# Three more units of w_out's product in rounded parts, and a new order of issue, in a fused attention and feed-forward kernel

## The chip, the core and the metric

The kernel runs on one core of a Trainium2 chip. The metric is the device time of one execution in microseconds (us). Before the change it was 151.05 us, the median of three runs (150.78 to 151.63). The engines are named as the profile names them: PE is TensorE, DVE is VectorE, ACT is ScalarE, POOL is GpSimd and SP is SyncE, which here issues every transfer.

## The reference

Two stages follow each other. The first is a linear attention with quadratic features, for 4 batches and 4 heads of 1088 tokens with 32 values each:

```python
phi(x) = outer(S1 @ x, S2 @ x)                    # 8 x 8 = 64 features
kv  = einsum('bhsf,bhsd->bhfd', phi(k), v);  z = phi(k).sum(tokens)
x   = (phi(q) @ kv) / (phi(q) @ z + 1e-6)         # heads side by side: 128 values a token
h    = relu(x @ w_in)                             # 1024 wide
conv = sum(conv_w[k] * h shifted by k - 1 tokens, k = 0, 1, 2)
out  = (h * sigmoid(conv)) @ w_out                # back to 128
```

[...]

## The kernel before

**The work.** All the tokens stand side by side, 4 x 1088 with a column of zeros between the batches, and are cut into nine segments (`SEGS`: 382, seven of 510, 404 columns). Each segment meets eight blocks of 128 of the 1024 hidden values, so there are 72 units, and the last two blocks of the last segment are halved: 74 units (`UNITS`), numbered segment by segment. Unit 8s + f is block f of segment s up to unit 69; 70 and 71 are the halves of block 6 of the last segment, 72 and 73 those of block 7.

**A unit** is a chain over the engines:

- `f_in:u` (PE, L1190 to L1192): three matmuls with rounded parts (whi by xhi, wlo by xhi, whi by xlo) into the PSUM bank `a`
- `f_relu:u` (ACT L1198 or DVE L1200): the ReLU, from `a` to `h` in SBUF
- `f_tapa:u`, `f_tapb:u` (DVE, L1204): the two outer taps of the convolution, added into `a`
- `f_gate:u` (ACT, L1211): the sigmoid
- `f_mul:u` (POOL, or DVE; L1215): `g` = `h` times the gate
- `f_out:u` (PE): `g` by a block of `w_out`, added up in the bank `o` over the eight units of a segment

`f_out` has two forms. The plain one (L1240) is one fp32 matmul, which the profile shows as two instructions. For the units in `THREE`, blocks 1, 4 and 6 (`PARTS`) of the segments 3 to 7, ACT first rounds `g` (`f_hi`, L1219), POOL takes the rest (`f_lo`, L1223), and PE runs three matmuls with rounded parts (L1230 to L1232): 15 units. After the eighth unit `f_copy` brings `o` to SBUF and `f_store` sends it out.

**Before the units** the attention makes `x`. Batch 0 goes by tokens: `q_ab:0:g`, `q_take`, `q_ac`, `q_sum`, `q_rec`, `q_div`, `q_phi` (POOL, L877), the transposes `q_t` (PE), `q_ttake`, then `q_x:0:1` (PE, L1148), whose result becomes `xhi` and `xlo` by `q_hi:0:0` and `q_lo:0:0` (DVE, L1166). The first `f_in` needs `q_lo:0:0`. The batches 1 to 3 go by features, through DRAM rows (`r_put`, `rep`) and products on POOL (`q_prod`, L1136). The weights are taken apart in quarters (`i:0` to `i:3` for `w_in`, `o:0` to `o:3` for `w_out`: the steps `low`, `e`, `m`, `f`, `clamp`, `power`, `sign`, `value`, and for `w_in` also `high` and `rest`).

**What sets the order.** The table `ORDER` (L86) writes out by hand, for every engine, the order of its steps, and so also which engine takes a step that two could take. Instructions of an engine are issued in that order and in no other. A planner, `schedule` (L488), goes through the table with costs and deals out buffers of a few pools by it (seven PSUM banks `p`, six `row` buffers and so on); it also puts in four warm-up matmuls ahead of PE's first step. SP issues a transfer once the eighth one before it has landed. The planner's guess of when a load lands (`landed`, L551 to L556) so enters the buffers dealt out and the sequence in which the engines' streams are recorded, but not the order within an engine.

Of the kernel before, what the change touches and what calls it, by code (L numbers as in the profile page):

```python
# [56 lines left out]
    for b in range(B)  # L57
# [40 lines left out]
        k_ab:1:0 k_ab:0:0 k_ab:1:1 s:turn k_ab:0:1 k_z:1 q_b:1 k_wz:1 k_ab:0:2 q_a:1 k_z:0 k_kv:0:0 k_wz:0 q_den:1
        k_f:3 k_kv:0:1 q_ab:0:0 k_ab:3:1 q_ab:0:1 k_f:2 k_kv:0:2 k_kv:1:0 k_kv:1:1 k_kvt:0 q_all:1 q_t:0:0:1 q_t:0:0:0
        k_ab:3:0 k_ab:2:1 q_t:0:1:1 q_t:0:1:0 q_ab:0:2 k_ab:2:0 k_kvt:1 q_x:0:1 k_z:2 k_kv:3:0 q_b:2 f_in:2 f_in:0  # L100
        f_in:3 k_wz:2 f_in:7 k_kv:3:1 q_a:2 f_in:1 q_t:0:2:0 f_in:6 q_t:0:2:1 q_den:2 k_kv:2:0 k_kv:2:1 q_x:0:2 f_in:4
# [12 lines left out]
    """,
    "ACT": """
        s:low i:0:low k_take:0:0 i:0:clamp i:0:power i:3:low k_wq:1 k_take:0:2 q_atake:1 i:3:clamp i:0:high i:3:power
        k_wq:0 o:0:clamp i:1:low o:0:power k_ftake:3 i:1:clamp i:3:high i:1:power q_take:0:0 k_take:3:1 oh:1:high
        q_take:0:1 k_ftake:2 i:1:high k_kvtwo:0 o:3:low i:2:low o:3:clamp o:3:power k_kvtake:0 i:2:clamp i:2:power
        q_ttake:0:0:0 k_take:3:0 k_take:2:1 o:2:low q_ttake:0:1:1 q_ttake:0:1:0 oh:6:high q_take:0:2 k_take:2:0
        k_kvtake:1 o:2:clamp q_hi:0:0 o:2:power q_btake:2 f_relu:2 f_relu:0 f_relu:3 k_wq:2 o:1:low f_relu:7 k_kvtwo:3  # L120
        f_gate:0 k_kvturn:3 i:2:high f_gate:2 f_relu:1 q_ttake:0:2:0 f_gate:3 q_eps:2 q_ttake:0:2:1 f_relu:6 f_gate:1
        f_gate:7 q_hi:0:2 f_relu:4 o:1:clamp f_relu:5 o:1:power f_gate:6 f_relu:14 f_gate:4 f_relu:8 f_gate:5
        f_relu:10 f_relu:9 f_gate:8 f_relu:13 oh:4:high f_relu:12 f_gate:9 k_kvtwo:2 k_kvtake:3 f_gate:10 f_copy:0:0
        f_gate:13 f_relu:11 f_gate:14 k_kvturn:2 q_hi:1:2 q_hi:1:3 q_hi:1:1 q_hi:1:0 f_gate:12 f_relu:15 f_gate:11
        f_relu:26 f_relu:25 f_relu:18 f_gate:15 f_relu:20 f_relu:17 f_relu:16 f_gate:26 f_gate:17 f_gate:16 f_relu:21
        f_gate:18 f_gate:25 f_relu:30 f_relu:19 f_gate:20 f_copy:1:0 f_relu:22 f_relu:23 f_gate:19 f_gate:21 f_hi:25
# [1197 lines left out]
```

## Time and profile before

| | |
|---|---|
| median of three runs | 151.05 us (150.78 to 151.63) |
| the profiled execution | 150.91 us |
| its span in the trace | 149.2 us |
| what lies around the span | 1.7 us |
| instructions on PE, DVE, ACT, POOL | 1116, 278, 252, 152 |
| PE clock granted | 1.0 |

The span is what the profile's rows show, from the first instruction to the last; the runs' times are some 1.7 us longer. Start times in the rows count from the span's start. Busy times of PE overlap, since matmuls are pipelined, so that the step from one start to the next tells more than a duration; for the other engines a step is some 0.1 us shorter than a duration.

### The profile page before, as it was taken

The page shows a single profiled execution, that of the slowest core. Times are in us where ns is not written, and L with a number is a line of the kernel's source. Part 1 is how long each engine was busy: PE and PEld are TensorE (multiplying, and loading weights), DVE is VectorE, ACT ScalarE, POOL GpSimd, SP SyncE. Part 2 cuts the span into 40 slices and gives each one's busy share as a digit, 9 for nine tenths or more (in the row PEclk, how much of TensorE's full clock was granted, in tenths as well). Part 3 has the DMA queues.
Part 4 walks back from the last instruction along what each step waited for, and adds up shares of the span by engine and source line. Part 5 has one row for each costly group of instructions (what it writes and reads, how often), then busy time and mean ns, then how long its engine had stood idle before and what let it go on. Part 6 is the DMA issues. An engine that isn't in the chain of part 4 may idle for free.

```text
span 149.2 us, 3306 instructions
## 1 busy us (share of the span) xinstructions
PE 143.1 (96%) x1116; PEld 96.1 (64%) x1116; DVE 136.9 (92%) x278; ACT 117.0 (78%) x252; POOL 135.4 (91%) x152
## 2 busy tenths in 40 slices
PE   7998897999999999999999999999999999999991
PEld 3486686776765486564547655765676776686780
DVE  1789999999999999999999999999999999999910
ACT  4054979799977986979797888799898898898621
POOL 7858999999999999998999989999999999999810
DMA  4999999699992670001339217700200010020021
GB/s 114 301 324 405 407 406 399 241 253 256 228 239 70 187 165 0 4 20 50 70 91 251 78 40 190 179 0 0 70 4 0 5 67 0 2 70 0 0 74 55
DMA packets 9233, 19.82 MB, mean 133 GB/s; under 512 B 1280, under 2 KB 5376, under 8 KB 9216
## 3 DMA queue, kind: packets, MB, share of 16 engines
q1 hardware_dynamic: 9216, 19.61, 43.3%
q8 instruction: 9, 0.15, 0.4%
q14 instruction: 8, 0.07, 0.2%
HBM read 15.70 MB, written 3.90 MB: 131 GB/s over the span
## 4 chain that ended last, share of the span: by engine, by line
PE 81%; DMA 10%; SPq 3%; ACT 3%; issue 0%; ACTq 0%
PE o L1240 31%; PE a L1190 12%; PE a L1191 11%; PE a L1192 11%; DMA rows<-in_w_in 5%; DMA vt<-in_v 5%; PE xps L1148 3%; PE o L1230 3%; PE o L1231 2%; PE o L1232 2%; PE qps L1022 2%; SPq L643 2%; PE kvps L968 1%; SPq L646 1%; PE qps L1076 1%; ACT e L762 1%
## 5 line engine op out<-in xcount | busy, mean ns | idle before, releaser
L1204 DVE SCALAR_TENSOR_TENSOR a<-h,ratio,a 128x510 f32<-128x510 f32 (+3 forms) x148 | 94.8, 706 | 0.4 <-ACT h L1198 0.2
L1215 POOL TENSOR_TENSOR g<-h,s 128x510 f32<-128x510 f32 (+3 forms) x57 | 68.3, 1222 | 3.7 <-PE o L1240 2.5
L1240 PE MATMUL o<-g,w_out_sb 128*128 128x510 f32 (+2 forms) x130 | 52.2, 517 | 0.0
L1211 ACT ACTIVATE s<-a,mid 128x510 f32<-128x510 f32 (+3 forms) x57 | 37.5, 666 | 6.5 <-DVE a L1204 4.7
L1198 ACT ACTIVATE h<-a 128x512 f32<-128x512 f32 (+3 forms) x71 | 39.0, 569 | 4.4 <-PE a L1192 2.2
L1190 PE MATMUL a<-xhi,whi 128*128 128x512 f32 (+3 forms) x74 | 37.4, 505 | 0.0
L1240 PEld LDWEIGHTS o<-g,w_out_sb 128*128 128x128 f32 x130 | 23.3, 189 | 9.8 <-issue 5.1
L1191 PE MATMUL a<-xhi,wlo 128*128 128x512 f32 (+3 forms) x74 | 28.0, 379 | 0.0
L1192 PE MATMUL a<-xlo,whi 128*128 128x512 f32 (+3 forms) x74 | 28.0, 378 | 0.0
L1190 PEld LDWEIGHTS a<-xhi,whi 128*128 128x128 f32 x74 | 13.9, 188 | 10.3 <-ACT s L1211 2.8
L1223 POOL TENSOR_TENSOR gg<-g,gg 128x510 fp32r<-128x510 f32 x15 | 19.2, 1288 | 0.6 <-ACT gg L1219 0.3
L1191 PEld LDWEIGHTS a<-xhi,wlo 128*128 128x128 f32 x74 | 14.0, 189 | 5.6 <-issue 3.5
L1136 POOL TENSOR_TENSOR rows<-rows 128x544 f32<-128x544 f32 x12 | 16.2, 1364 | 0.0
L1192 PEld LDWEIGHTS a<-xlo,whi 128*128 128x128 f32 x74 | 13.9, 188 | 2.5
L877 POOL TENSOR_TENSOR kp<-kab 128x768 f32<-128x768 f32 (+2 forms) x6 | 11.7, 1958 | 2.6 <-ACT kab L615 1.7
L1211 ACT ACTIVATE a<-a,mid 128x510 f32<-128x510 f32 (+3 forms) x17 | 10.5, 623 | 1.8 <-DVE a L1204 1.8
L1215 DVE TENSOR_TENSOR g<-h,a 128x510 f32<-128x510 f32 (+3 forms) x17 | 10.6, 626 | 0.7 <-PE o L1240 0.6
L1219 ACT CAST gg<-g 128x510 fp32r<-128x510 f32 x15 | 9.4, 627 | 0.2 <-DVE g L1215 0.2
L1230 PE MATMUL o<-gg,ohi 128*128 128x510 f32 x15 | 8.7, 578 | 0.0
L615 ACT COPY out<-o 128x510 f32<-128x510 f32 (+2 forms) x10 | 5.2, 524 | 4.3 <-PE o L1240 4.3
L732 ACT ACTIVATE f<-rows 128x256 f32<-128x256 uint32 x7 | 3.1, 448 | 4.3 <-DMA rows<-in_w_in 4.2
L717 PE MATMUL warm<-w_out_sb 128*128 128x512 f32 x8 | 5.4, 838 | 1.1 <-POOL above L676 1.1
(127 smaller groups left out, 178.7 us busy)
## 6 DMA issues: line engine op xcount, KB each, us to landing
...
```

The source lines that it names most:

```text
L877: e.tensor_tensor(out=out.rearrange("p c (h i j) -> p (c h) i j", i=R, j=R), in0=a.unsqueeze(3).broadcast_to([P, n, R, R]), in1=b.unsqueez ...
L1136: mul(on["q_prod", b, pr, c])(out=st["rep", 0][:, pr, cols], in0=st["rep", 0][:, pr, cols], in1=st["rep", 1][:, pr, cols], op=ALU.mult)
L1190: nc.tensor.matmul(a[:, : n + 2], whi[:, w], xhi[:, x], start=True, stop=False)
L1191: nc.tensor.matmul(a[:, : n + 2], wlo[:, w], xhi[:, x], start=False, stop=False)
L1192: nc.tensor.matmul(a[:, : n + 2], whi[:, w], xlo[:, x], start=False, stop=True)
L1198: nc.scalar.activation(h[:, : n + 2], a[:, : n + 2], AF.Relu)
L1204: nc.vector.scalar_tensor_tensor(out=a, in0=h[:, k : n + k], scalar=ratio[:, f, k : k + 1], in1=a, op0=ALU.mult, op1=ALU.add)
L1211: nc.scalar.activation(s, a, AF.Sigmoid, scale=mid[:, f : f + 1])
L1215: mul(on["f_mul", u])(out=gt[:, :n], in0=st["h"][:, 1 : n + 1], in1=st["s"], op=ALU.mult)
L1223: mul(on["f_lo", u])(out=gg[:, 1], in0=st["g"][:, :n], in1=gg[:, 0].bitcast(F32), op=ALU.subtract)
L1230: nc.tensor.matmul(to, ohi[:, i], gg[:, 0], start=f == 0, stop=False)
L1240: nc.tensor.matmul(acc[g, p][:, : hi - lo], w_out_sb[:, f * P : (f + 1) * P], st["g"][:, lo - c0 : hi - c0], start=f == 0, stop=f == NF - 1,)
```

## The change

It has three parts.

**Three more units in rounded parts.** `THREE` now begins at segment 2, so the units 17, 20 and 22 (510 columns each) get an `f_hi` and an `f_lo`, and their `f_out` has the three-matmul form: 18 units in all.

**The planner's guess.** A load that the planner takes to be through between 16.5 and 30 us counts as landed 0.6 us later. No instruction comes from this alone.

**A new order.** All five lists of `ORDER` are new; the steps are the same but for the three `f_hi` and `f_lo`. Forty-two steps change engines. DVE takes over eight `f_mul` (8, 13, 29, 30, 51, 58, 64, 72) and gives POOL five (9, 43, 62, 65, 67); it takes five `f_relu` (23, 31, 50, 67, 69) and gives ACT three (24, 33, 66); it takes `i:0:low`, `i:1:low`, `i:3:low`, `o:2:low`, `q_atake:1`, `q_eps:2`, `k_take:3:0`, `k_kvtake:1` and the last `f_copy`, and gives ACT or POOL `k_take:1:0`, `s:take`, `o:0:low`, `q_btake:1`, `q_atake:2`, `q_hi:0:1`, `q_ttake:0:0:1`, `q_eps:1`, `q_eps:3`, `k_wq:3` and `oh:4:rest`. The units are no longer begun in the same sequence within a segment, and on SP the loads of `v3` and `o2` come earlier, those of `i2` and `v2` later. The line numbers of what follows `ORDER` are two higher (L1204 is now L1206).

```diff
     "SP": """
-        dma:k2 dma:v1 dma:o3 dma:i2 r_put:1:0:b dma:v2 dma:o2 dma:q0.2 r_put:1:3:b dma:v3 dma:q2 r_put:1:2:b
+        dma:k2 dma:v1 dma:o2 dma:o3 dma:v3 r_put:1:3:b r_put:1:2:b dma:q0.2 dma:i2 r_put:1:0:b dma:q2 r_put:1:1:b
...
-THREE = [u for u, (s, f, c0, n) in enumerate(UNITS) if f in PARTS and 3 <= s < NSEG - 1]
+THREE = [u for u, (s, f, c0, n) in enumerate(UNITS) if f in PARTS and 2 <= s < NSEG - 1]
...
-            landed.append(wire + 450)
-            lat = wire + 450 - t
+            there = wire + 450 + 600 * (16500 < wire < 30000)
+            landed.append(there)
+            lat = there - t
```

Three places show how the lists moved. The first is DVE's stream behind the preparation of the small weights (`ratio` is its last result). `kab<-kps` is a `k_take`, `kp<-kab,kps` is `k_phi:1:1`, and the rows of 128x256 take `w_in` apart. Before:

```order
L847 TENSOR_TENSOR ratio<-small,least 128x24
L615 COPY kab<-kps 128x320
L739 TENSOR_SCALAR e<-rows 128x256
L744 TENSOR_SCALAR m<-rows 128x256
L747 SCALAR_TENSOR_TENSOR f<-m,f 128x256
L615 COPY kab<-kps 128x2x128
L767 SCALAR_TENSOR_TENSOR w<-rows,e 128x256
L615 COPY s2t<-s_213 128x128
```

And with the change:

```order
L849 TENSOR_TENSOR ratio<-small,least 128x24
L617 COPY kab<-kps 128x2x128
L879 TENSOR_TENSOR kp<-kab,kps 128x1024
L746 TENSOR_SCALAR m<-rows 128x256
L617 COPY kab<-kps 128x2x96
L741 TENSOR_SCALAR e<-rows 128x256
L736 TENSOR_SCALAR f<-rows 128x256
```

The first copy on DVE is now the shorter `k_take:1:1`, the outer product follows it at once, and a `low` step (L736) stands on DVE where ACT had it; the copy of 320 columns and that of `s2t` are gone from DVE.

The second place is the end of DVE's stream. `g<-h,a` is an `f_mul` on DVE, `h<-a` an `f_relu`; 404 columns belong to whole units of the last segment, 202 to its halves. Before, the last rows are:

```order
L1204 SCALAR_TENSOR_TENSOR a<-h,ratio,a 128x404
L1204 SCALAR_TENSOR_TENSOR a<-h,ratio,a 128x202 x2
L1215 TENSOR_TENSOR g<-h,a 128x404
L1204 SCALAR_TENSOR_TENSOR a<-h,ratio,a 128x202
L1215 TENSOR_TENSOR g<-h,a 128x404
L1215 TENSOR_TENSOR g<-h,a 128x202
```

With the change they are:

```order
L1217 TENSOR_TENSOR g<-h,a 128x404
L1202 TENSOR_SCALAR h<-a 128x406
L1206 SCALAR_TENSOR_TENSOR a<-h,ratio,a 128x202
L1206 SCALAR_TENSOR_TENSOR a<-h,ratio,a 128x404
L1217 TENSOR_TENSOR g<-h,a 128x202
L1206 SCALAR_TENSOR_TENSOR a<-h,ratio,a 128x404
L1206 SCALAR_TENSOR_TENSOR a<-h,ratio,a 128x202 x3
L1217 TENSOR_TENSOR g<-h,a 128x404
L1217 TENSOR_TENSOR g<-h,a 128x202
L617 COPY out<-o 128x202
```

In both, the product of 404 columns that stands last but one among the products is `f_mul:69`, and the one of 202 columns behind it is `f_mul:73`; the last `f_relu` is now `f_relu:69`, a few rows ahead of it, and the copy of a finished half to the output has come to DVE behind everything else. PE's list ends in both with `f_out:69` and then the four halves.

The third place is SP's list of transfers behind the load of `k2` (`in_kT`, 128x1088). Before:

```order
L636 DMA vt_73<-in_v 128x1152
L646 DMA rows<-in_w_out 128x512
L646 DMA rows<-in_w_in 128x512
L1118 DMA far<-r 32x3x272
L636 DMA vt_74<-in_v 128x1152
L646 DMA rows<-in_w_out 128x512
L643 DMA rows<-in_qT 128x320
L1118 DMA far<-r 32x3x272
L636 DMA vt_75<-in_v 128x1152
L643 DMA rows<-in_qT 128x1088
```

With the change:

```order
L638 DMA vt_73<-in_v 128x1152
L648 DMA rows<-in_w_out 128x512 x2
L638 DMA vt_75<-in_v 128x1152
L1120 DMA far<-r 32x3x272 x2
L645 DMA rows<-in_qT 128x320
L648 DMA rows<-in_w_in 128x512
L1120 DMA far<-r 32x3x272
L645 DMA rows<-in_qT 128x1088
```

`q0.2` (`in_qT`, 128x320) had one quarter of `w_in` ahead of it that it no longer has, and one more `r_put`; `q2` (`in_qT`, 128x1088) no longer has `v2` (`vt_74`) ahead of it. `v2` now follows `q3`.

More of the change, by code (lines that the diff above doesn't have):

```diff
@@ L96 @@
+        f_store:6:0 f_store:7:0 f_store:8:0 f_store:8:1
     """,
     "PE": """
[L98 to L101, printed above, removed]
@@ L117 @@
[L117 to L121, printed above, removed]
@@ L122 @@
[L122 to L126, printed above, removed]
@@ L137 @@
-        f_relu:61 f_gate:72 f_relu:67 f_gate:64 f_relu:63 f_gate:61 f_relu:69 f_gate:67 f_relu:73 f_relu:70 f_gate:63
-        f_gate:69 f_gate:73 f_gate:70 f_copy:7:0 f_copy:8:1 f_copy:8:0
+        s:low k_take:1:0 k_take:0:0 s:take i:3:clamp i:3:power i:0:clamp q_btake:1 k_wq:1 o:0:low i:0:power k_take:0:2
+        o:0:clamp o:0:power i:0:high k_wq:0 i:1:clamp k_ftake:3 i:3:high i:1:power oh:1:high q_take:0:0 k_take:3:1
+        q_take:0:1 q_eps:1 i:1:high k_ftake:2 k_kvtwo:0 o:3:low o:2:clamp o:2:power o:3:clamp k_kvtake:0 o:3:power
@@ new lines @@
+        k_take:2:0 q_ttake:0:0:1 k_kvturn:1 q_ttake:0:0:0 q_ttake:0:1:1 q_ttake:0:1:0 k_take:2:1 i:2:low q_take:0:2
+        q_hi:0:0 i:2:clamp q_hi:0:1 i:2:power oh:6:high o:1:low q_btake:2 f_relu:0 f_relu:3 k_wq:2 f_relu:7 f_relu:1
+        f_gate:0 f_gate:3 oh:4:high k_kvtwo:3 q_atake:2 k_kvturn:3 f_relu:6 q_ttake:0:2:1 f_relu:2 f_gate:7 i:2:high
+        q_ttake:0:2:0 f_gate:1 f_gate:6 o:1:clamp k_kvtwo:2 o:1:power q_hi:0:2 k_kvtake:3 f_relu:5 f_gate:2 f_relu:4
+        k_kvturn:2 f_relu:8 f_gate:5 f_relu:9 f_gate:4 f_relu:14 f_relu:11 f_relu:13 f_gate:8 f_relu:12 f_gate:14
@@ new lines @@
+        f_gate:9 f_copy:0:0 q_hi:1:2 q_hi:1:3 f_gate:12 f_relu:10 f_gate:11 f_relu:15 k_wq:3 f_gate:10 q_hi:1:1
+        q_hi:1:0 f_gate:13 q_btake:3 q_atake:3 f_gate:15 f_relu:24 f_relu:17 f_relu:20 f_relu:16 f_gate:24 f_relu:18
+        f_gate:17 f_gate:20 f_relu:19 f_gate:16 f_hi:17 f_gate:18 f_relu:26 f_hi:20 f_copy:1:0 f_relu:22 f_gate:19
+        f_relu:21 q_eps:3 f_gate:23 f_relu:27 f_gate:22 f_relu:25 f_gate:21 f_gate:27 f_relu:30 f_hi:22 f_relu:28
+        f_gate:25 f_gate:26 k_kvtake:2 f_gate:30 q_hi:2:1 q_hi:2:0 f_relu:29 f_gate:28 f_hi:25 f_copy:2:0 f_relu:34
@@ L139 @@
     """,
     "DVE": """
-        s:m s:e s:f s:clamp s:power s:sign s:value taps k_take:1:0 i:0:e i:0:m i:0:f k_take:1:1 i:0:sign s:take
-        k_take:0:1 i:3:m k_zmask:1 i:3:f k_phi:1:1 o:0:low q_btake:1 o:0:m i:3:e k_zmask:0 q_m:1 o:0:f o:0:e i:3:sign
-        q_eps:1 i:1:e i:1:m o:0:sign i:1:f k_phi:0:2 i:1:sign q_ac:0:0 q_rec:1 q_sum:0:0 q_ac:0:1 q_rec:0:0 q_sum:0:1
-        q_div:0:0 q_rec:0:1 q_div:0:1 o:3:m o:3:e o:3:f i:2:e k_kvtwo:1 i:2:m o:3:sign q_ttake:0:0:1 i:2:sign q_div:1
-        k_phi:3:0 i:2:f o:2:e o:2:m q_ac:0:2 o:2:f q_sum:0:2 k_zmask:2 q_rec:0:2 q_lo:0:0 o:2:sign q_hi:0:1 q_div:0:2
@@ L175 @@
[L175 removed]
+        ones ident wqs s:four k_phi:1:0 k_phi:0:0 i:0:value k_phi:0:1 i:3:value o:0:value i:0:rest i:3:rest i:1:value
+        oh:1:rest q_wide:1 q_phi:0:0 q_phi:0:1 k_phi:2:0 i:1:rest o:3:value k_phi:3:1 q_phi:0:2 o:2:value i:2:value
+        f_mul:0 k_phi:2:1 f_mul:7 i:2:rest f_mul:1 f_mul:6 o:1:value f_mul:2 oh:4:rest f_mul:3 q_wide:2 oh:6:rest
+        q_prod:1:0:0 q_prod:1:1:1 q_prod:1:0:1 f_mul:14 q_prod:1:1:0 f_mul:9 f_mul:12 f_mul:11 f_mul:10 q_prod:2:0:0
```

120 lines of the change are left out of this document (62 added, 58 removed).

## The prediction

> **What bounds the kernel now.** I read the page first, then the busy times by stretch, then the chain of waits, and last the timelines of the start and the end. The page has three engines above 90%, so the whole span does not say which one binds:
>
> ```profile
> PE 143.1 (96%) x1116; PEld 96.1 (64%) x1116; DVE 136.9 (92%) x278; ACT 117.0 (78%) x252; POOL 135.4 (91%) x152
> ```
>
> The stretches do. The columns are the stretch in us, then the busy us of PE, weight loads, DVE, ACT and POOL:
>
> ```profile
> 20.00:28.20 8.20, 7.41 (x186) 5.54 (x181) 7.92 (x22) 7.51 (x23) 8.20 (x8) 1.00 1.00 386
> 28.20:60.00 31.80, 31.80 (x300) 22.10 (x297) 31.59 (x62) 27.00 (x63) 31.33 (x29) 1.00 0.69 170
> 60.00:100.00 40.00, 40.00 (x190) 24.16 (x189) 39.76 (x66) 34.08 (x65) 38.92 (x33) 1.00 0.34 91
> 100.00:143.00 43.00, 43.00 (x196) 29.52 (x195) 42.27 (x74) 37.71 (x75) 40.22 (x34) 1.00 0.06 19
> ```
>
> From 28.2 us on PE is never idle, and DVE is idle for 0.21 + 0.24 + 0.73 = 1.2 us of 114.8. POOL is idle for 0.5 + 1.1 + 2.8 = 4.3 us by the unrounded rows, ACT for 16. So two engines run without a break side by side, and the end is set by the one that has more left. At the end the timeline shows which:
>
> ```profile
> 141.49 0.57 DVE L1215 TENSOR_TENSOR g<-h,a 128x404 f32<-128x404 f32 x1
> ...
> 141.50 4.45 PE L1240 MATMUL o<-g,w_out_sb 128*128 128x510 f32 x22
> ...
> 142.64 0.37 DVE L1215 TENSOR_TENSOR g<-h,a 128x202 f32<-128x202 f32 x1 [0.58 <-PE o L1240]
> ...
> 143.37 0.61 POOL L1215 TENSOR_TENSOR g<-h,s 128x202 f32<-128x202 f32 x1 [2.01 <-PE o L1240]
> ...
> 146.04 0.33 ACT L615 COPY out<-o 128x202 f32<-128x202 f32 x1 [0.40 <-PE o L1240]
> ```
>
> DVE makes f_mul:69 at 141.49 and is done at 143.0, while PE works off 22 instructions: f_out:63, then 67, 68, 69 and the four halves. PE is the last, by a little.
>
> **The three units on PE.** The chain of waits has the price of both forms:
>
> ```profile
> 67.93 3.42 PE o L1240 x8
> ...
> 110.11 0.23 PE o L1230
> 110.35 0.23 PE o L1231
> 110.58 0.23 PE o L1232
> 110.81 0.24 PE a L1190
> ```
>
> Eight instructions in 3.42 us are four plain units, 0.855 each; the other form takes 110.81 - 110.11 = 0.70. Three units save 3 x 0.155 = 0.47 us of PE. Row against rule: the Trainium skill's page "FP8 and Floating Point Precision", section "TensorE Precision Notes", counts four passes for a true fp32 matmul; four of the 0.233 us passes would be 0.93, and the saving 0.69. The row stands, and nothing below uses 0.69.
>
> By 0.855 for f_out:63 and 0.69 for each whole unit of 404 columns (0.855 x 404 / 510 = 0.68, and a second pair), f_out:69 starts in before at 141.50 + 0.855 + 1.38 = 143.74. From there to the last copy at 146.04 are 2.30 us. Since f_out:69 and four halves end PE's list before and after, this 2.30 stays, and the question is when f_out:69 can start: when PE gets there, or when DVE has finished f_mul:69.
>
> **The same three units on POOL and ACT.**
>
> ```profile
> L1215 POOL TENSOR_TENSOR g<-h,s 128x510 f32<-128x510 f32 x45 | 57.5, 1300 | 1.4 <-ACT s L1211 0.8 <-PE o L1240 0.2
> ...
> L1223 POOL TENSOR_TENSOR gg<-g,gg 128x510 fp32r<-128x510 f32 x15 | 19.2, 1288 | 0.6 <-ACT gg L1219 0.3 <-DVE a L1204 0.3
> ...
> L1219 ACT CAST gg<-g 128x510 fp32r<-128x510 f32 x15 | 9.4, 627 | 0.2 <-DVE g L1215 0.2
> ```
>
> POOL gains 3 x 1.29 = 3.9 us. It gives DVE eight f_mul for five: six of 510 columns for three, which is 3 x 1.30 = 3.9 less, and one each of 404 and 202 for two of 404, which is some 0.4 more (half a product of 404, and the 202 above takes 0.61). oh:4:rest comes and k_kvturn:1 goes, both small. So POOL has about 0.4 more. ACT gains 3 x 0.63 = 1.9 for f_hi and loses two f_relu of about 0.6. Both lie in the idle 4.3 and 16 us, so I count them at nothing; uncovered, they would cost 0.4 and 0.7.
>
> **DVE** pays for it. Steps from start to start:
>
> ```profile
> 116.67 0.68 DVE L1215 TENSOR_TENSOR g<-h,a 128x510 f32<-128x510 f32 x1
> 117.26 8.53 DVE L1204 SCALAR_TENSOR_TENSOR a<-h,ratio,a 128x510 f32<-128x510 f32 x14
> ...
> 126.84 0.57 DVE L1200 TENSOR_SCALAR h<-a 128x406 f32<-128x406 f32 x1
> 127.33 1.73 DVE L1204 SCALAR_TENSOR_TENSOR a<-h,ratio,a 128x404 f32<-128x404 f32 x3
> 128.97 0.57 DVE L1215 TENSOR_TENSOR g<-h,a 128x404 f32<-128x404 f32 x1
> 129.45 11.31 DVE L1204 SCALAR_TENSOR_TENSOR a<-h,ratio,a 128x510 f32<-128x510 f32 x20
> ```
>
> A step is 0.09 less than a duration: an f_mul of 510 is 0.59, of 404 0.48, of 202 0.37 - 0.09 = 0.28; an f_relu of 406 is 0.49, and of 512 I take 0.59, as for f_mul. Eight f_mul come, 6 x 0.59 + 0.48 + 0.28 = 4.30; five go, 3 x 0.59 + 2 x 0.48 = 2.73. Five f_relu come, 3 x 0.59 + 2 x 0.49 = 2.75; three go, 2 x 0.59 + 0.49 = 1.67. That is +2.65 us. The small steps of the start bring some back. Prices by the same subtraction:
>
> ```profile
> L744 DVE TENSOR_SCALAR m<-rows 128x256 int32<-128x256 int32 x8 | 3.3, 419 | 0.1
> ...
> L615 DVE COPY r<-qps 128x272 f32<-128x272 f32 x2 | 0.9, 430 | 0.0
> ...
> L615 DVE CAST xhi<-xps 128x384 fp32r<-128x384 f32 x1 | 0.6, 554 | 0.0
> L615 DVE COPY qt<-qtps 128x384 f32<-128x384 f32 x1 | 0.6, 551 | 0.0
> L615 DVE COPY kab<-kps 128x320 f32<-128x320 f32 x1 | 0.5, 493 | 0.9 <-PE kps L915 0.9
> ...
> L734 DVE TENSOR_SCALAR f<-rows 128x256 f32<-128x256 uint32 x1 | 0.3, 292 | 0.0
> ```
>
> q_hi:0:1 and q_ttake:0:0:1 go (0.46 each), q_btake:1 and q_atake:2 (0.34 each) for q_atake:1 (0.34), k_take:1:0 for k_take:3:0 (0.40 both), one low step for four (0.20 each), and five little steps for two (s:take, q_eps, k_wq, k_kvtake, oh:4:rest, 128 columns or fewer; an estimate of 0.1 to 0.2 each, below the low step's), some -0.4. Sum: -0.92 - 0.34 + 0.60 - 0.4, about -1.1. So DVE has 1.55 us more ahead of f_mul:69. The last f_copy stands behind it.
>
> DVE also starts earlier. Its first copy waited 0.9 us for ten matmul instructions of k_ab:1:0; k_ab:1:1 has eight:
>
> ```profile
> 6.59 2.86 PE L915 MATMUL kps<-small,rows 128*128 128x64 f32 x24
> ```
>
> Two times 2.86 / 24 = 0.24 us. With the idle time of before, f_mul:69 ends at 141.49 + 0.57 + 1.55 - 0.24 = 143.37.
>
> **The start of the units.** The rows of before:
>
> ```profile
> 24.69 0.88 PE L1009 MATMUL qps<-wq,rows 128*128 128x96 f32 x6 [0.79 <-ACT f L732]
> ...
> 26.00 0.88 PE L1148 MATMUL xps<-qt,kv 64*32 64x384 f32 x16
> ...
> 27.50 0.50 DVE L1166 TENSOR_TENSOR xlo<-xps,xhi 128x384 fp32r<-128x384 f32 x1
> ...
> 28.23 0.44 PE L1190 MATMUL a<-xhi,whi 128*128 128x384 f32 x1
> ```
>
> PE's 0.79 us of idling at 24.69 is q_ab:0:2; ACT's step, named there, is no input of it, so I read it as the wait for q0.2. At the 386 GB/s of the stretch from 20 to 28.2 us, 256 KB fewer and 102 KB more ahead of q0.2 bring it some 0.4 us earlier, and q2, with 576 KB fewer and one r_put more, some 1.2. Against this stands POOL: oh:1:rest (0.4) now precedes q_wide:1 and q_phi, while the 0.7 us that POOL idled ahead of k_phi:0:1 shrinks little; and ACT now has o:2 and o:3's steps before q_ttake, so that it waits for both quarters. The bounds are 0.6 us earlier (PE waits for nothing but q0.2 and q2) and no gain. I take 0.4: f_in at 27.8.
>
> **The sum.** PE alone reaches f_out:69 at 143.74 - 0.47 - 0.4 = 142.87. DVE allows it at 143.37, and a little more: the walk through the new list shows two or three waits in its first 15 us (i:3:sign for ACT's i:3:power, now behind two copies; q_ac:0:1 for q_take:0:1; o:3's steps for their load), 0.2 to 0.6 us; I take 0.3. Then 143.7, against 143.74: nothing is left of PE's gain. The forecast is the profiled execution's own **150.9 us**, 0.1 below the median of the runs. What a measurement of this kernel can tell from no change is about 0.5%: below 150.3 or above 151.8.
>
> **Rivals.**
>
> *PE sets the end (0.24).* Then f_out:69 starts at 142.87, 0.87 earlier: 150.0 us, or 149.8 with the full 0.6 at the start. For it speaks that PE has not idled since 28.2; against it that f_mul:69 would have to end by 142.8, which takes 0.6 of DVE's few idle tenths away, not 0.3 more.
>
> *The start is not earlier, and DVE is late by its whole growth (0.26).* If the load of o3, or ACT's six conversion steps behind it, keep q_ttake where it was, q_lo:0:0 starts at 27.5 as before. Behind it DVE has the 2.65, three i:2 steps of 0.33 (the first row above) and two little ones more (1.25), and o:2:sign, q_hi:0:1, q_atake:2, k_wq:3 and oh:4:rest less (1.4): 2.5 us. Then f_mul:69 ends at 142.06 + 2.5 = 144.56, f_out:69 starts 0.8 to 0.9 late, and the time is 151.8 us; half a microsecond later at the start makes it 152.2. It decides once q_lo:0:0 starts after about 26.6: from there on each tenth is a tenth at the end.
>
> *POOL is held up by DVE's low steps (0.04).* Three more of them stand on DVE in POOL's busiest stretch. If each stopped POOL for its 0.29 us, q_phi would come 0.9 later and the units with it, and by the arithmetic of the last rival the time would be 151.8 or more. The one such step of before stood beside this product on POOL, the first row:
>
> ```profile
> 12.84 0.78 POOL L774 TENSOR_TENSOR wv<-w,f 128x256 f32<-128x256 f32 x1
> ...
> 15.80 0.74 POOL L774 TENSOR_TENSOR wv<-w,f 128x256 f32<-128x256 f32 x1
> ```
>
> It is longer by 0.04, so I give the rival little. The Trainium skill's page "SBUF — State Buffer", section "SBUF: two separate sides", has the rule: a DVE operation in a two-port mode and a GpSimd operation exclude each other for a whole instruction. No row of before shows a full stop.
>
> *The planner's 0.6 us changes something by itself.* It can't move an instruction within an engine; it may deal out other buffers. I give it no chance of its own.
>
> **How the numbers follow.** The likeliest case has the remaining 0.46. Its own range is 150.4 to 151.5: f_mul:69 0.5 earlier or 0.6 later. The range of all reaches from 149.8, where PE sets the end, to 152.2, the late start. Faster by over 0.5% is nearly all of the first rival and no other, 0.23; slower takes two thirds of the second, the third and a little of the likeliest, 0.25; no change 0.52.
>
> **What would show it.** Right: L1230 has 18 instructions, the idle time of DVE after 28 us stays near 1.2 us, f_mul:69 ends between 143.3 and 144.2, and PE waits shortly before f_out:69, where it did not wait. The first xlo on DVE would start near 26.7 and the first f_in between 27.4 and 27.8. Wrong: PE idle in the middle of the units (a late f_mul or f_lo, which no sum of mine sees), a first xlo after 27.5, or DVE idle for more than 2 us.

## The result, and the profile after

The changed kernel took 153.48 us, the median of five runs (152.11 to 153.83), against 151.1 before (five runs, 150.78 to 153.34); the ratio, which is not the quotient of the medians, is 1.0131, with a 95% interval of 1.0086 to 1.0175. Six further runs gave 152.44 us and a ratio of 1.0104 (1.0056 to 1.0153). The medians here and below are of all executions, while the ratios leave out nine slow ones of four kernels below (eight of 153.7 to 155.3 us, one of 204.65). So the changed kernel is slower by some 1%, and the forecast of 150.9 us with the range 149.8 to 152.2 was wrong. The profiled execution took 153.75 us with a span of 152.0. Of the eleven executions six have a mean clock of 0.978 to 0.989 and all but one of these took 153.3 to 153.8 us, while the other five, at 1.0, took 151.9 to 152.5; the trace shown first has the lower clock.

The engines on the page of the changed kernel, as in the prediction's first fence:

```profile
PE 145.5 (96%) x1119; PEld 98.1 (65%) x1119; DVE 140.6 (92%) x281; ACT 118.1 (78%) x256; POOL 135.7 (89%) x151
```

The stretches of the changed kernel follow (PE, weight loads, DVE, ACT, POOL, then the granted clock), with two stretches of the start in front:

```profile
6.00:20.00 14.00, 12.03 (x169) 8.38 (x167) 11.37 (x30) 5.79 (x17) 8.12 (x12) 0.88 1.02 380
14.00:16.00 2.00, 2.00 (x18) 1.37 (x21) 2.00 (x7) 1.59 (x6) 0.13 (x2) 0.50 1.07 420
20.00:28.20 8.20, 7.81 (x163) 6.78 (x163) 7.96 (x24) 7.30 (x24) 8.20 (x10) 1.00 0.93 317
28.20:60.00 31.80, 31.65 (x389) 20.86 (x388) 31.48 (x67) 27.60 (x69) 31.69 (x30) 1.00 0.79 191
60.00:100.00 40.00, 40.00 (x176) 25.61 (x175) 39.97 (x65) 35.51 (x67) 38.40 (x32) 1.00 0.32 85
100.00:143.00 43.00, 43.00 (x191) 28.85 (x190) 42.75 (x73) 37.17 (x73) 42.44 (x36) 1.00 0.06 19
```

And the first of them before the change:

```profile
6.00:20.00 14.00, 12.96 (x238) 10.00 (x240) 12.78 (x42) 8.08 (x24) 11.56 (x19) 1.00 1.01 375
```

From 28.2 us on PE and DVE run almost without a break, as they did. Most of the loss lies in the first 20 us. There DVE finished 30 instructions instead of 42, POOL 12 instead of 19, and between 14 and 16 us PE ran at a clock of 0.50. The timeline of that stretch shows it in single rows (start, duration, then what the instruction waited for in brackets):

```profile
10.15 2.40 POOL L879 TENSOR_TENSOR kp<-kab 128x1280 f32<-128x1280 f32 x1 [2.80 <-ACT kab L617]
...
11.04 1.66 DVE L736 TENSOR_SCALAR f<-rows 128x256 f32<-128x256 uint32 x1
...
13.22 1.00 DVE L736 TENSOR_SCALAR f<-rows 128x256 f32<-128x256 uint32 x1
...
13.44 0.41 PE L958 MATMUL wzps<-zt,s2t 128*128 128x64 f32 x2 [1.62 <-DVE zt L952]
...
15.94 0.73 POOL L776 TENSOR_TENSOR wv<-w,f 128x256 f32<-128x256 f32 x1 [1.87 <-DVE w L769]
...
28.74 0.88 PE L1150 MATMUL xps<-qt,kv 64*32 64x384 f32 x16
...
30.17 0.56 DVE L1168 TENSOR_TENSOR xlo<-xps,xhi 128x384 fp32r<-128x384 f32 x1
...
30.87 0.45 PE L1192 MATMUL a<-xhi,whi 128*128 128x384 f32 x1
```

The two rows of L736 are `i:3:low` and `i:0:low`, two of the four `low` steps that the change gave to DVE; a `low` step turns the low 32 bits of a quarter's 64-bit weights into numbers (`f<-rows`). They take 1.66 and 1.00 us; the same instruction took 0.29 before. Both stand beside a product of POOL that is under way (L879: `k_phi:1:0`, then `k_phi:0:0`), and both end some 0.15 us after it. Behind them PE waits 1.62 us and POOL 1.87, and the first `xlo` and the first `f_in` come at 30.17 and 30.87 instead of 27.50 and 28.23. The end of the timeline carries the delay on unchanged:

```profile
145.94 3.16 PE L1242 MATMUL o<-g,w_out_sb 128*128 128x202 f32 x17
...
146.16 0.99 DVE L1217 TENSOR_TENSOR g<-h,a 128x404 f32<-128x404 f32 x2
...
149.18 0.33 ACT L617 COPY out<-o 128x202 f32<-128x202 f32 x1 [2.43 <-PE o L1242]
```

From the first `f_in` to the last copy are 149.18 - 30.87 = 118.31 us, and before 146.04 - 28.23 = 117.81. So of the 3.14 us by which the last copy is later, 2.64 were lost ahead of the first `f_in`; 0.59 of these had arisen by DVE's first copy, at 8.52 instead of 7.93.

### The profile page after: what moved, and what is told of

Read it like the earlier page. It is cut to its first block, busy times and chain, and to the rows that moved or that the text cites. A ratio compares the mean times of both kernels' runs of the same rounds, so it can differ in the third digit from the quotient of the medians.

```text
span 152.0 us, 3330 instructions
## 1 busy us (share of the span) xinstructions
PE 145.5 (96%) x1119; PEld 98.1 (65%) x1119; DVE 140.6 (92%) x281; ACT 118.1 (78%) x256; POOL 135.7 (89%) x151
## 4 chain that ended last, share of the span: by engine, by line
PE 87%; POOL 5%; DVE 3%; ACT 2%; issue 1%; POOLq 0%; ACTq 0%; DVEq 0%
PE o L1242 29%; PE a L1192 12%; PE a L1193 10%; PE a L1194 10%; PE warm L719 4%; PE xps L1150 3%; PE qps L1024 3%; PE o L1232 3%; PE o L1234 3%; PE o L1233 3%; POOL qp L879 2%; PE kps L917 1%; PE kvps L970 1%; DVE f L736 1%; PE qtps L1107 1%; POOL kp L879 1%
## 5 line engine op out<-in xcount | busy, mean ns | idle before, releaser
L1206 DVE SCALAR_TENSOR_TENSOR a<-h,ratio,a 128x510 f32<-128x510 f32 (+3 forms) x148 | 94.2, 704 | 0.3 <-ACT h L1200 0.2
L1217 POOL TENSOR_TENSOR g<-h,s 128x510 f32<-128x510 f32 (+3 forms) x54 | 65.0, 1218 | 3.7 <-ACT s L1213 2.9
L1242 PE MATMUL o<-g,w_out_sb 128*128 128x510 f32 (+2 forms) x124 | 49.6, 513 | 0.0
L1213 ACT ACTIVATE s<-a,mid 128x510 f32<-128x510 f32 (+3 forms) x54 | 35.7, 670 | 5.7 <-DVE a L1206 4.8
L1225 POOL TENSOR_TENSOR gg<-g,gg 128x510 fp32r<-128x510 f32 x18 | 23.1, 1287 | 0.0
L879 POOL TENSOR_TENSOR kp<-kab 128x1280 f32<-128x1280 f32 (+2 forms) x6 | 11.7, 1962 | 4.0 <-ACT kab L617 2.8
L1213 ACT ACTIVATE a<-a,mid 128x510 f32<-128x510 f32 (+3 forms) x20 | 12.5, 625 | 2.2 <-DVE a L1206 2.1
L1217 DVE TENSOR_TENSOR g<-h,a 128x510 f32<-128x510 f32 (+3 forms) x20 | 12.3, 622 | 0.1
L1221 ACT CAST gg<-g 128x510 fp32r<-128x510 f32 x18 | 11.2, 634 | 0.1
L617 ACT COPY kab<-kps 128x320 f32<-128x320 f32 (+2 forms) x6 | 2.3, 386 | 7.1 <-PE kps L917 7.1
L1233 PE MATMUL o<-gg,olo 128*128 128x510 f32 x18 | 7.1, 394 | 0.0
```

What stands on the lines that cost most here:

```text
L879: e.tensor_tensor(out=out.rearrange("p c (h i j) -> p (c h) i j", i=R, j=R), in0=a.unsqueeze(3).broadcast_to([P, n, R, R]), in1=b.unsqueez ...
L1206: nc.vector.scalar_tensor_tensor(out=a, in0=h[:, k : n + k], scalar=ratio[:, f, k : k + 1], in1=a, op0=ALU.mult, op1=ALU.add)
L1213: nc.scalar.activation(s, a, AF.Sigmoid, scale=mid[:, f : f + 1])
L1217: mul(on["f_mul", u])(out=gt[:, :n], in0=st["h"][:, 1 : n + 1], in1=st["s"], op=ALU.mult)
L1225: mul(on["f_lo", u])(out=gg[:, 1], in0=st["g"][:, :n], in1=gg[:, 0].bitcast(F32), op=ALU.subtract)
L1242: nc.tensor.matmul(acc[g, p][:, : hi - lo], w_out_sb[:, f * P : (f + 1) * P], st["g"][:, lo - c0 : hi - c0], start=f == 0, stop=f == NF - 1,)
```

## The experiments

**The theories.** *The lock*: a `low` step on DVE (tensor_scalar, SBUF to SBUF) waits until the product that POOL is working at is done, and what hangs on DVE's stream starts late. *The order*: the new order itself brings the units late, and the long `low` steps only fill a wait that would be there anyway. *The clock*: PE's lower clock is the loss. *DVE's load*: the units' pace is DVE's, whatever the start does.

Each trace splits into three: up to DVE's first copy (`kab<-kps`), which varies by itself from 7.6 to 8.75 us (below); from there to the first `f_in`, called *start* here; and from there to the last copy, called *stream*. The median beside the first trace is of five runs, the repeated kernel's and that with added matmuls of six, that of the kernel before with one step moved of eight, and the others of twelve; the ratio is to the kernel before on the same chip. The last three columns come from one trace each.

| kernel | median us | ratio, 95% | DVE's first copy | start | stream |
|---|---|---|---|---|---|
| before | 151.0 | | 7.93 | 20.30 | 117.8 |
| after, first trace | 153.48 | 1.0086 to 1.0175 | 8.52 | 22.35 | 118.3 |
| after, again | 152.44 | 1.0056 to 1.0153 | 8.07 | 21.61 | 118.2 |
| low in another form | 152.04 | 1.0032 to 1.0091 | 8.49 | 20.66 | 118.95 |
| four low on ACT | 150.36 | 0.9940 to 0.9981 | 7.82 | 19.94 | 118.1 |
| two low on ACT | 151.73 | 1.0003 to 1.0063 | 8.10 | 21.22 | 117.9 |
| two low early on DVE | 151.27 | 0.9994 to 1.0042 | 7.88 | 20.63 | 119.5 |
| before, one low moved | 153.32 | 1.0066 to 1.0145 | 8.19 | 21.98 | 118.4 |
| matmuls in PE's gap | 152.54 | 1.0068 to 1.0138 | 8.59 | 21.61 | 117.9 |
| four low on ACT, three warm-ups | 150.68 | 0.9943 to 0.9988 | 7.60 | 20.17 | 117.9 |
| four low on ACT, 15 units | 151.9 | 1.0025 to 1.0074 | 7.77 | 19.71 | 119.5 |
| four low on ACT, DVE relieved | 151.62 | 1.0007 to 1.0059 | 7.72 | 20.37 | 118.6 |
| before, `v2` later | 151.12 | 0.9981 to 1.0025 | 8.75 | 19.22 | 118.3 |
| before, planner's guess | 150.91 | 0.9971 to 1.0011 | 8.37 | 20.32 | 117.9 |

The four kernels with the four `low` steps on ACT have the same order at the start, and their starts still lie between 19.71 and 20.37. So a start in the table is good to some 0.3 us. It lies near before's 20.3 in all four, and 1.2 us or more below the changed kernel's.

### The changed kernel again

The kernel is the changed one, without an edit.

> The changed kernel once more, for a second trace of it. In the first trace PE's eight warm-up instructions took 6.58 us instead of 5.42, PE ran at a clock of 0.5 between about 14 and 17 us, and the time was 153.75 us; two other runs of it show a clock of 1.0 and 152.1 to 152.2 us. If the clock is one cause beside another (the theory of the lock: DVE's steps of the form low wait until a product of POOL is done), a trace with a clock of 1.0 still shows the first two low steps on DVE (128x256) with 1 to 1.7 us each instead of 0.3, the first xlo at about 28.6 and the first f_in about 1.1 us later than before's 28.23. If the clock is all (rival), the low steps take 0.3 us in such a trace. If neither, the start is late in the order itself, and the first xlo is late with short low steps and a full clock.

This trace has a clock of 1.0, and took 152.45 us. The timeline has the same two rows, with the same durations, beside the same product:

```profile
9.70 2.40 POOL L879 TENSOR_TENSOR kp<-kab 128x1280 f32<-128x1280 f32 x1 [2.34 <-ACT kab L617]
...
10.59 1.66 DVE L736 TENSOR_SCALAR f<-rows 128x256 f32<-128x256 uint32 x1
...
12.77 1.00 DVE L736 TENSOR_SCALAR f<-rows 128x256 f32<-128x256 uint32 x1
```

POOL's product ends at 12.10 and the step at 12.25. PE waits as long as in the first trace, and its clock stays at 1.00 behind the wait (the second row is a stretch, as above):

```profile
12.99 0.41 PE L958 MATMUL wzps<-zt,s2t 128*128 128x64 f32 x2 [1.62 <-DVE zt L952]
...
14.00:16.00 2.00, 1.63 (x59) 1.07 (x58) 1.97 (x7) 1.47 (x4) 0.51 (x1) 1.00 1.06 415
```

The first `f_in` comes at 29.68, 1.45 us later than before. So the lock is there without the lower clock, and in the first trace the clock came on top.

### The same steps in a form that takes one operand from PSUM

```diff
-nc.vector.tensor_scalar(st["f"], lo, 2.0**-52, 1.0, op0=ALU.mult, op1=ALU.add)
+nc.vector.scalar_tensor_tensor(out=st["f"], in0=lo, scalar=2.0**-52,
+    in1=<e or m of the same quarter, in PSUM>, op0=ALU.mult, op1=ALU.min)
 # and in m, for these quarters, the 1.0 of the sum:
-0xFFFFF, None, op0=ALU.bitwise_and
+0xFFFFF, 0x100000, op0=ALU.bitwise_and, op1=ALU.bitwise_or
```

The order stays, but for `o:2:low`, which goes behind its neighbour `o:2:e`.

> The changed kernel with the same steps on the same engines in the same order, but the four low steps on DVE in another form (scalar_tensor_tensor with its second operand in PSUM; the 1.0 is put in by the step m instead, so that the sum is the same). Theory of the lock: the low steps take 0.4 us wherever POOL stands, i:0:sign and the first xlo come 1 to 2 us earlier than in the changed kernel, and the time is 150.5 to 151.3 us in executions at full clock. Rival, the order itself makes the start late: the low steps were only waiting for what would have been waited for anyway, and the time stays within 0.3 us of the changed kernel's.

```profile
10.11 2.40 POOL L897 TENSOR_TENSOR kp<-kab 128x1280 f32<-128x1280 f32 x1 [2.75 <-ACT kab L627]
...
11.13 0.42 DVE L749 SCALAR_TENSOR_TENSOR f<-rows,e 128x256 f32<-128x256 uint32 x1
...
12.07 0.40 DVE L749 SCALAR_TENSOR_TENSOR f<-rows,m 128x256 f32<-128x256 uint32 x1
```

On the same engine, at the same place and beside the same product of POOL (10.11 to 12.51) the steps take 0.42 and 0.40 us: it is the form, and not the place, that waits. The start shrinks from 21.61 to 20.66. The time falls less, to 152.04, short of the 150.5 to 151.3 expected, and its interval overlaps the changed kernel's. In the trace the stream is 0.75 us longer than in the repeated one, and that arises between `f_out:12` and `f_out:18`; the other buffers that the planner deals out for this form may do it, which wasn't tried.

### The four steps on ACT

```diff
     "ACT": """
-        s:low k_take:1:0 ... k_wq:0 i:1:clamp ... k_kvtwo:0 o:3:low
+        s:low i:0:low i:3:low k_take:1:0 ... k_wq:0 i:1:low i:1:clamp ... k_kvtwo:0 o:2:low o:3:low
     "DVE": """
-        ... i:3:low ... i:0:low ... i:1:low ... o:2:low ...
```

> The changed kernel with the four low steps given back to ACT (i:0:low and i:3:low ahead of its first copies, where it stood idle until 9.6 us; i:1:low and o:2:low later). Theory of the lock: as with the other form, first xlo 1 to 2 us earlier, 150.3 to 151.3 us at full clock, and DVE has 0.8 us less to do. Rival, the order: within 0.3 us of the changed kernel. If DVE's load and not the start sets the end, this kernel gains 0.8 us and the other form nothing.

The rows of its start and of its end:

```profile
7.83 0.43 ACT L737 ACTIVATE f<-rows 128x256 f32<-128x256 uint32 x1 [4.06 <-DMA rows<-in_w_in]
...
8.45 0.44 ACT L737 ACTIVATE f<-rows 128x256 f32<-128x256 uint32 x1 [0.18 <-DMA rows<-in_w_in]
...
27.15 0.55 DVE L1171 TENSOR_TENSOR xlo<-xps,xhi 128x384 fp32r<-128x384 f32 x1
...
27.76 0.44 PE L1195 MATMUL a<-xhi,whi 128*128 128x384 f32 x1
...
142.79 0.99 DVE L1220 TENSOR_TENSOR g<-h,a 128x404 f32<-128x404 f32 x2
...
145.82 0.33 ACT L620 COPY out<-o 128x202 f32<-128x202 f32 x1 [2.43 <-PE o L1245]
```

The first two steps lie in time that ACT spent idle. The start falls to 19.94 us, near before's 20.30, and the time to 150.36 us. That is 2.1 us less than the changed kernel's 152.44, and a little faster than the kernel before: the ratio is 0.996 (0.994 to 0.9981). With everything else of the change in place, this version beats both. Of the 1.67 us of start between the two, the other form brings 0.95, where no step waits, and the absence of the steps from DVE's stream the other 0.72; the two steps ahead of `i:0:sign` take 0.82 us there. With starts good to 0.3 us, this split is a rough one.

### One such step added to the kernel before

```diff
     "ACT": """
-        ... k_take:0:0 i:0:clamp i:0:power i:3:low k_wq:1 ...
+        ... k_take:0:0 i:0:clamp i:0:power k_wq:1 ...
     "DVE": """
-        ... i:3:m k_zmask:1 ...
+        ... i:3:m i:3:low k_zmask:1 ...
```

> The kernel before with one step moved: i:3:low from ACT to DVE, right behind i:3:m, where POOL works at k_phi:1:0 (10.47 to 12.87 in the trace of before). Theory of the lock: the step takes until POOL's product is done, 1.5 to 1.9 us instead of 0.3, and k_phi:1:1 and what follows on DVE come that much later; since PE waited 0.79 us for q0.2 ahead of the units, the time rises by 0.3 to 1.3 us. Rival, the kernel after is late for its order and the lock is harmless: the step takes 0.3 us or the time stays within 0.3 us of before's 151.0.

```profile
11.46 1.82 DVE L736 TENSOR_SCALAR f<-rows 128x256 f32<-128x256 uint32 x1
...
13.56 0.41 PE L958 MATMUL wzps<-zt,s2t 128*128 128x64 f32 x2 [2.33 <-DVE zt L952]
```

One step of 0.3 us takes 1.82, PE idles for 2.33 us behind it, and the kernel before becomes 153.32 us, as slow as the changed one: the ratio is 1.0105 (1.0066 to 1.0145). I had expected at most 1.3 us; it is 2.3. Six of eight executions have a clock of 0.978 to 0.989 and took 153.2 to 155.3 us, while the two at full clock took 152.4, which is 1.4 more than before. The step alone can thus cost all that the change lost.

### Two steps moved ahead of POOL's products; two steps left beside them

```diff
     "DVE": """
-        ... taps k_take:1:1 k_phi:1:1 i:0:m k_take:0:1 i:3:e i:3:low i:0:e k_zmask:1 i:0:low ...
+        ... taps k_take:1:1 i:0:low i:3:low k_phi:1:1 i:0:m k_take:0:1 i:3:e i:0:e k_zmask:1 ...
```

> The changed kernel with i:0:low and i:3:low still on DVE and in their first form, but both put right behind DVE's first copy, where POOL has nothing to do yet (its first product starts some 1.6 us after that copy). Theory of the lock: they take 0.3 us each there, the first f_in comes 19.9 to 20.7 us behind DVE's first copy (21.6 in the changed kernel, 20.3 before), and the time is 150.4 to 151.2 us. Rival, the steps cost what they cost because DVE's start is too full, wherever they stand: 21.3 us or more, and the time stays within 0.4 us of the changed kernel's 152.4.

```profile
8.22 0.29 DVE L739 TENSOR_SCALAR f<-rows 128x256 f32<-128x256 uint32 x1
...
8.76 0.29 DVE L739 TENSOR_SCALAR f<-rows 128x256 f32<-128x256 uint32 x1 [0.26 <-DMA rows<-in_w_in]
...
9.50 2.40 POOL L882 TENSOR_TENSOR kp<-kab 128x1280 f32<-128x1280 f32 x1 [2.15 <-ACT kab L620]
```

Ahead of POOL's first product the same form takes 0.29 us. The start is 20.63, at the upper edge of what I expected, with `i:1:low` still waiting (0.72 us), and the median of 151.27, just above the 151.2 expected, is 1.2 below the changed kernel's. The long stream of 119.5 belongs to the profiled execution, which took 152.59 us and was the slowest of the twelve: PE idles there once for 1.65 us at 40.4.

The other kernel gives only `i:0:low` and `i:3:low` to ACT and leaves `i:1:low` and `o:2:low` on DVE.

```diff
     "ACT": """
-        s:low k_take:1:0 ...
+        s:low i:0:low i:3:low k_take:1:0 ...
```

> The changed kernel with only i:0:low and i:3:low given to ACT; i:1:low and o:2:low stay on DVE beside POOL's later products. If the first two carry the whole cost, the time is within 0.3 us of the 150.4 us of the kernel with all four on ACT, and the first f_in comes 20 to 20.3 us behind DVE's first copy. If each step that meets a product of POOL costs its wait, i:1:low (0.72 us in the second trace of the changed kernel) adds 0.4 to 0.9 us: 150.8 to 151.3 us.

```profile
21.08 1.51 POOL L882 TENSOR_TENSOR qp<-qn,qab 128x768 f32<-128x768 f32 x1
21.11 1.63 DVE L739 TENSOR_SCALAR f<-rows 128x256 f32<-128x256 uint32 x1
```

`o:2:low` meets `q_phi:0:0` 0.03 us after that has started, and waits for all of it. In the changed kernel's second trace the two began within 0.01 us of each other; there the step took 0.28 us and POOL's product 1.66 instead of 1.51, so that POOL lost 0.15. So the cost of each step depends on where POOL stands when it comes up; the kernel takes 151.73 us, 1.4 more than with all four on ACT and more than I gave it.

### The clock

```diff
 # in k_wz, for batch 1, ahead of the matmul that waits for zt
+for _ in range(3):
+    nc.tensor.matmul(ps[:, :256], idle, <idle twice>, start=True, stop=True)
```

> The changed kernel with three added matmuls of zeros (256 columns each, into the bank that the next matmul writes anew) on PE ahead of k_wz:1, where PE stood idle for 1.6 us before its clock fell to 0.5. Theory that the idle time lowers the clock: no execution shows a clock under 1.0, the runs lie at 152.0 to 152.4 us, and nothing else moves. Rival: the clock falls as before in some of the runs, and the runs again come in two kinds 1.5 us apart. The lock stays, so the time is not expected under 151.8 us.

The matmuls stand in the gap, and none of the six executions has a clock below 0.997:

```profile
11.82 1.56 PE L959 MATMUL wzps<-w_out_sb 128*128 128x256 f32 x6
...
13.51 0.41 PE L961 MATMUL wzps<-zt,s2t 128*128 128x64 f32 x2
```

The time is 152.54 us, 152.06 to 153.24. The `low` steps take 1.66 and 1.00 us and the start 21.61, as in the repeated trace. So PE's idle time behind the lock brings the lower clock: six of eleven executions have it without the matmuls, none of six with them, and none of 23 executions of the kernel before on the same chip has a clock under 0.996. (Single executions of two kernels without this wait, the other form and the 15 units, have one of 0.989, so it is not the only way there.) What the lower clock costs is less clear. The first trace's start is 0.74 us longer than the second's, and the changed kernel's executions with the lower clock took 1.4 us more in the median than those without. But the six with the added matmuls have a mean of 152.64 us and the six of the repeated kernel 152.63, and two of the former took over 153 at full clock, which I had not expected. So taking the lower clock away won nothing that these runs show. The second experiment on the clock takes one of the four warm-up matmuls away from the kernel with the four steps on ACT.

```diff
-FIRST = 4
+FIRST = 3
```

> The kernel with the four low steps on ACT, with three warm-up matmuls ahead of PE's first step instead of four. In four traces PE's warm-up instructions are 0.85 us apart until some point between 4.5 and 7.0 us, different in each, and 0.43 apart behind it, and the first k_ab waits for the last of them although its operands are there by 6.4 us. Theory that this spreads the times: the first k_take on DVE starts at 7.4 to 7.9 us in every execution, and the time falls by 0.2 to 0.7 us with a smaller spread. Rival: with less warm-up the slow spacing lasts into the k_ab instructions, and the time is the same or rises by up to 1 us.

It took 150.68 us (150.1 to 151.27), within the other's 150.08 to 151.12. DVE's first copy comes at 7.60, but the units are no earlier (first `f_in` at 27.77) and the spread is as wide. The expectation failed; what else spreads the runs by 1 us is open.

### The three units, DVE's load, and the two small parts

The three units go back to the plain form in the kernel with the four steps on ACT.

```diff
-THREE = [u for u, (s, f, c0, n) in enumerate(UNITS) if f in PARTS and 2 <= s < NSEG - 1]
+THREE = [u for u, (s, f, c0, n) in enumerate(UNITS) if f in PARTS and 3 <= s < NSEG - 1]
 # and f_hi:17 f_hi:20 f_hi:22 leave ACT's list, f_lo:17 f_lo:20 f_lo:22 POOL's
```

> The kernel with the four low steps on ACT, without the three added units in rounded parts: 17, 20 and 22 go back to the plain product, and their f_hi and f_lo are left out. If PE sets the pace from the first f_in to the end, the time rises by the 0.41 to 0.47 us that three plain units cost more, to 150.8 us. If DVE's load sets it, the time is the same within 0.1 us. If POOL's 3.9 us for the three f_lo cost waits in the middle, it falls.

It took 151.9 us, 1.5 more. The units begin 0.28 us earlier than in its base, and the last copy comes 146.97 - 145.82 = 1.15 later. PE's starts show that `f_out:17`, `f_out:20` and `f_out:22` take 0.15 us more each, and that most of the rest arises in two places: 0.33 behind unit 22, where DVE waits 1.01 us and POOL idles, and 0.58 at the start of segment 5.

```profile
77.96 0.69 DVE L1225 TENSOR_TENSOR g<-h,a 128x510 f32<-128x510 f32 x1 [1.01 <-PE o L1250]
...
78.85 1.30 POOL L1225 TENSOR_TENSOR g<-h,s 128x510 f32<-128x510 f32 x1 [1.48 <-PE o L1250]
```

An order fitted to the one form loses more than PE's 0.45 when the units go back. The next kernel relieves DVE near the end, again in the kernel with the four steps on ACT.

```diff
     "ACT": """
-        ... f_gate:66 f_relu:70 ...
+        ... f_gate:66 f_relu:69 f_relu:70 ...
     "DVE": """
-        ... f_tapb:72 f_mul:64 f_relu:69 f_tapa:70 f_tapa:69 f_mul:72 f_tapb:69 ...
+        ... f_tapb:72 f_tapa:70 f_tapa:69 f_tapb:69 ...
     "POOL": """
-        ... f_mul:65 f_mul:66 f_mul:68 f_mul:70
+        ... f_mul:65 f_mul:64 f_mul:66 f_mul:68 f_mul:72 f_mul:70
```

> The kernel with the four low steps on ACT, with DVE relieved near the end: f_mul:64 and f_mul:72 go to POOL and f_relu:69 to ACT, 1.25 us of DVE's work ahead of f_mul:69. If PE's unbroken stream sets the end, as its steps of 0.69 from f_out:63 to f_out:69 without a gap suggest, the time stays within 0.2 us of that kernel's 150.4 (or rises by 0.1 to 0.5 if a product on POOL is then late for its f_out). If f_mul:69 on DVE sets it, as the prediction had it, f_out:69 comes up to 0.6 us earlier and the time falls to 149.8 to 150.1 us.

```profile
140.90 3.52 PE L1247 MATMUL o<-g,w_out_sb 128*128 128x202 f32 x19 [0.28 <-POOL g L1222]
...
142.83 0.57 DVE L1222 TENSOR_TENSOR g<-h,a 128x404 f32<-128x404 f32 x1
```

`f_mul:69` is done at 143.40, and `f_out:69` starts at 144.43, 0.68 behind `f_out:68` like every unit there: PE sets the end even when DVE is a microsecond early. Against its base PE loses 0.44 us ahead of `f_out:64` and 0.11 ahead of `f_out:65`, behind the products moved to POOL, and the units began 0.33 later. The time is 151.62, 1.26 more than the base's and more than the 0.5 that I allowed for a late product.

The last two try one part of the change alone on the kernel before. The first is a transfer, that of `v2`.

```diff
     "SP": """
-        ... r_put:1:0:b dma:v2 dma:o2 dma:q0.2 ... dma:q3 dma:o1 ...
+        ... r_put:1:0:b dma:o2 dma:q0.2 ... dma:q3 dma:v2 dma:o1 ...
```

> The kernel before with one transfer moved: the load of v2 (590 KB) behind q3, so that q0.2 and q2 have it no longer ahead of them. It tries the prediction's step that the start of the units hangs on q0.2: then q0.2 lands about 1.4 us earlier, PE's 0.79 us of idling ahead of q_ab:0:2 goes, the first f_in comes 0.4 to 0.6 us earlier and the time falls by as much, to 150.4 to 150.6 us. Rival, the wait only moves to the next step (q_ttake on ACT, POOL's q_phi): the first f_in stays within 0.2 us and so does the time.

It took 151.12 us against 151.01, ratio 1.0003 (0.9981 to 1.0025). In the trace `q0.2` lands at 22.77 us instead of 24.55, and `q_ab:0:2`, which before started 0.14 behind the landing, starts 1.77 behind it: that wait was real, and is gone. But the first `f_in` comes only 0.26 us earlier, at 27.97, less than expected. DVE's first copy stands at 8.75 in this trace, which makes the start look 1.1 us shorter, and the stream is 0.5 longer (118.3). The median did what the rival said; what holds the units instead is not settled. The second is the planner's guess.

```diff
-            landed.append(wire + 450)
-            lat = wire + 450 - t
+            there = wire + 450 + 600 * (16500 < wire < 30000)
+            landed.append(there)
+            lat = there - t
```

> The kernel before with only the planner's changed guess for when loads land (0.6 us later between 16.5 and 30 us). The order on each engine is the same; what can differ is which buffer a step is given. If it does nothing by itself, the time is within 0.3 us of before's 151.0. Rival, other buffers bring other waits: the difference is over 0.3 us either way.

It took 150.91 us, ratio 0.9991 (0.9971 to 1.0011): nothing, as expected.

## Why the prediction was wrong

**The step that failed is the start of the units.** The prediction had them 0.4 us earlier, at 27.8, with bounds of 0.6 earlier and none; they came 2.64 later in the first trace and 1.45 in the second. The sum for that start asked what PE, the loads, POOL and ACT would do, and had no term for DVE's `low` steps; in DVE's own sum they stood at 0.20 us each, from one row of 0.29. They took 1.66, 1.00, 0.33 and 0.40 us, or 1.66, 1.00, 0.72 and 0.28. With the first `xlo` at 30.17 and 28.98, the prediction's own sign of being wrong, a start after 27.5, had come. Take the four steps off DVE, and the first `f_in` comes at 27.76 (27.48 to 28.09 with the three kernels built on that one), as forecast. Of the reasons given for an earlier start, `q0.2` does land earlier, at 23.3 and 23.5 us in the changed kernel's two traces against 24.55; how much each reason brings is not shown.

**The third rival had the mechanism, the wrong loser and a chance of 0.04.** It asked what POOL loses to DVE's step, 0.29 us a time. POOL started first, and so DVE lost, up to the whole product. The row against it, a product of POOL of 0.78 us instead of 0.74, was the wrong one of two. Before, the step came up at the end of the long product ahead of that one:

```profile
9.00 3.87 POOL L877 TENSOR_TENSOR kp<-kab 128x768 f32<-128x768 f32 x2 [1.66 <-ACT kab L615]
...
12.73 0.29 DVE L734 TENSOR_SCALAR f<-rows 128x256 f32<-128x256 uint32 x1
```

POOL's second product ends at 9.00 + 3.87 = 12.87, and `o:0:low` at 13.02, 0.15 behind it, as the waiting steps do after. Only 0.14 us of the product were left when the step started, so that its 0.29 us show no wait. That there was no full stop in the trace showed only that no such step had yet met a product with more to go. The Trainium skill's page "SBUF — State Buffer", section "SBUF: two separate sides", which the prediction cited, says that whichever starts first keeps the pair of ports for the whole instruction. The traces agree: each waiting step ended some 0.15 us after POOL's product. The same page of the Trainium skill, in the section "Who interferes with whom", exempts a DVE instruction with at most one SBUF input outside the two-port modes, and the other form, with 0.42 and 0.40 us beside a running product, bears that out.

The kernel's source had the matter in hand as well. Its planner lets a step marked for it wait until the other of DVE and POOL is free (`port`, L526 and L527 before the change), and marks POOL's products so; but `low` is priced by `c_copy` (L211), whose form for DVE has no such mark. The planner, like the prediction, let `low` run beside POOL.

**The second rival gave 151.8 to 152.2 us** and comes near to the executions at full clock, by luck: it kept the start at 27.5 and made DVE late by its load. From the first `xlo` to the start of `f_mul:69` the changed kernel needs 146.16 - 30.17 = 115.99, before 141.49 - 27.50 = 113.99: 2.0 us more, where that rival said 2.5. But that is no loss by itself, as the next point shows.

**What sets the end.** The sum had `f_mul:69` at 143.37 and a little more, and PE at 142.87, so that DVE would decide. In the kernel with the four steps on ACT `f_mul:69` ends at 142.79 + 0.57 = 143.36, and `f_out:69` starts at 143.43. For DVE the agreement is partly luck, since this kernel's DVE lacks the four `low` steps, 0.80 us of the sum. PE's number was 0.6 too early. From the first `f_in` to the last matmul, PE's steps for the product with `w_out` add up to 48.5 us against 49.0 before, which is the gain that was forecast; but all its other steps add up to 69.1 against 68.4, and why is open. From `f_out:64` to `f_out:69` its instructions start 0.17 us apart without a gap. The first step behind that is 0.26, and 0.17 where DVE was relieved by 1.25 us, so `f_mul:69` held PE up by at most 0.09 us. So the first rival's statement, PE sets the end, is right but for that, at a time that the kernel with the four steps on ACT reached: 150.4 instead of the rival's 150.0.

**PE's gain of 0.47 us** is right for the units themselves (0.15 each, where they were put back), as are the idle cover of POOL (by the stretches it still idles 0.1 + 1.6 + 0.6 = 2.3 us of 114.8), the 2.30 us from `f_out:69` to the last copy (2.39), and the planner's share of nothing. **DVE's 1.55 us more** was somewhat too much. The groups of the changed kernel give the busy time of the `low` steps:

```profile
L1232 PE MATMUL o<-gg,ohi 128*128 128x510 f32 x18 | 9.9, 549 | 0.0
...
L736 DVE TENSOR_SCALAR f<-rows 128x256 f32<-128x256 uint32 x4 | 3.4, 848 | 0.0
```

DVE's busy time rose by 140.6 - 136.9 = 3.7, of which their waiting is 3.4 - 4 x 0.29 = 2.2; 1.5 are left, and 0.37 of these are the last `f_copy`, which the sum left out. So it is 1.1 by durations. The first row counts the 18 units.

**The clock** was in no rival. A late `k_zmask` leaves PE idle for 1.62 us at 11.8, and in the first trace a granted clock of 0.50 follows from about 14 to 17 us. The second trace, which has the same wait without the lower clock, has a start shorter by 0.74. So of the 2.64 us lost in the first trace 0.59 lie ahead of DVE's first copy, 0.74 go with the lower clock, and 1.31 (21.61 - 20.30) are left for the waiting steps; the four kernels with these steps on ACT win that back.
